# A GroupNorm streamed through one DMA queue: the pairs of stores and loads shifted by one tile

## The chip, the cores and the metric

The kernel runs on one core of a Trainium2 chip. The metric is the device time of one execution in microseconds (us); lower is better. The time before is the median of three runs.

## The reference

GroupNorm over `x` of shape (128, 1024, 32, 16) in bf16, with 32 groups of 32 channels:

```python
xr = x.reshape(B, G, C // G, H, W)          # 128, 32, 32, 32, 16
mu = xr.mean(axis=(2, 3, 4), keepdims=True)
var = ((xr - mu) ** 2).mean(axis=(2, 3, 4), keepdims=True)
xn = (xr - mu) / jnp.sqrt(var + 1e-5)
return xn.reshape(B, C, H, W) * g[None, :, None, None] + b[None, :, None, None]
```

Each of the 128 x 32 (sample, group) pairs has 32 x 512 = 16,384 values. The input is 134.2 MB and so is the output.

## The kernel before

**Tiles.** A tile holds 4 samples with all 32 groups: 128 partitions (one per sample and group) with 16,384 bf16 values each, 4.19 MB. There are 32 tiles (`NT`) and six buffers `xt0` to `xt5` (`NBUF`). Tile i uses buffer i mod 6. A tile is loaded into its buffer, scaled in place there, and stored from it.

**What is done with a tile.** The five engines each run a program of their own and meet through semaphores:

- TensorE (PE) adds the tile up: 32 matmuls with an identity matrix accumulate its 32 pieces of 512 columns in PSUM (line 148), after a wait for the load.
- VectorE (DVE) turns that into the negative mean (`mean`, line 165).
- ScalarE (ACT) computes the sum of squares in two activations over halves of the tile (line 278), then the standard deviation (lines 292 and 299).
- DVE makes the reciprocal, a scale and a bias for each channel (lines 179, 182, 189).
- DVE scales channels 0 to 13 in place and GpSimd (POOL) channels 14 to 31 (both line 218).

DVE's step for tile i begins with the mean of tile i + 1 and only then goes on to tile i:

```python
if i + 1 < NT:
    mean(i + 1, c + 3)
dve.reciprocal(out=col(rstd, i), in_=col(std, i))._wait_ge(...)
```

Engine instructions are issued in order, so the scaling of tile i also waits for the load of tile i + 1 and for its matmuls.

**What sets the order of the transfers.** All loads and stores of tiles are issued by SyncE (SP) on one queue, in the order of `sync_program`. SP issues them one after the other; where one has to wait, everything behind it in SP's program waits too. A store (line 123) waits until DVE and POOL have scaled the tile. A load (line 115) of tile n, from n = 6 on, waits until the store of tile n - 6 has landed, since it overwrites that buffer. The program first issues six loads, then goes through the stores in order; after each odd store (`RUN` is 2) it issues two loads.

Of the kernel before, what the change touches and what calls it, by code (L numbers as in the profile page):

```python
# [17 lines left out]
NBUF = 6  # L18
RUN = 2
# [5 lines left out]
def kernel(  # L25
# [15 lines left out]
    NT = B0 // NS  # L41
# [68 lines left out]
    def sync_program(sync):  # L110
        def load(i):
            j = i % NBUF
            if i >= NBUF:
                sync.wait_ge(st[j], 16 * (i // NBUF))
            sync.dma_start(out=xt[j][:], in_=x_v[i]).then_inc(ld[j], 16)

        for i in range(min(NBUF, NT)):
            load(i)
        for i in range(NT):
            j = i % NBUF  # L120
            sync.wait_ge(s_dve, i + 1)
            sync.wait_ge(s_pool, i + 1)
            sync.dma_start(out=o_v[i], in_=xt[j][:]).then_inc(st[j], 16)
            if i % RUN == RUN - 1:
                first = i + 1 + NBUF - RUN
                for n in range(first, min(first + RUN, NT)):
                    load(n)
        for j in range(NBUF):
            sync.wait_ge(st[j], 16 * len(range(j, NT, NBUF)))
# [179 lines left out]
    with tc.tile_critical():  # L309
        with nc.Block() as block:  # L310
            block.sync(sync_program)
            block.tensor(tensor_program)
            block.vector(vector_program)
            block.gpsimd(pool_program)
            block.scalar(scalar_program)
# [30 lines left out]
```

## Time and profile before

| | |
|---|---|
| median of 3 runs | 634.19 us (633.79 to 635.87) |
| the profiled execution | 634.93 us, its span 633.2 us |
| DMA queue of the tiles (q1) | 268.44 MB, 98.9% of the span |
| ACT busy | 476.5 us (75%) |
| POOL busy | 453.7 us (72%) |
| DVE busy | 348.3 us (55%) |
| PE busy | 259.3 us (41%) |
| a load, issue to landing | median 19.4 us (13.4 to 60.7) |
| a store, issue to landing | median 29.3 us (12.9 to 38.7) |

The span runs from the first to the last instruction in the profile; the device time holds 1.7 us more around it. Landing is when a transfer's completion reaches its semaphore. A transfer issued while others are queued waits for them, which is why most take two or three times as long to land as the queue needs for one. In a timeline of SP, a row gives the start of the first issue, the time to the end of the last issue of the row, and how many issues of one kind it merges.

### The profile page before, as it was taken

What the parts mean: (1) busy time and instruction counts of PE and PEld (TensorE: products, weight loads), DVE (VectorE), ACT (ScalarE), POOL (GpSimd) and SP (SyncE); (2) the same over time, 40 slices, a digit from 0 to 9 for tenths busy, and PEclk for the clock granted to TensorE, in tenths of its full rate; (3) what the DMA queues carried; (4) which work ended last, traced back from release to release, by engine and by line L of the source; (5) the groups of instructions that cost most, each with busy time, mean ns of one, the idle gap of its engine ahead of it and who ended that gap; (6) DMA issues with size and microseconds to landing.
All of it is one profiled execution on the core that took longest, in us unless ns stands there. A gap on an engine that the chain in (4) does not pass through costs nothing. (4 is left out here: it accounts for less than half of the span.)

```text
span 633.2 us, 3721 instructions
## 1 busy us (share of the span) xinstructions
PE 259.3 (41%) x1025; PEld 105.8 (17%) x1025; DVE 348.3 (55%) x610; ACT 476.5 (75%) x194; POOL 453.7 (72%) x583
## 2 busy tenths in 40 slices
PE   0977409054180632707327082360823608145000
PEld 0333103021030210302113031120301203012000
DVE  0057777767657175661757617476274762737660
ACT  0499999999959398693976939779397793967900
POOL 0049999999949398593986939769397693977990
PEclk9988858668595685957859577595765957659555
DMA  8999999999999999999999999999999999999986
GB/s 361 429 431 419 431 420 412 435 435 441 431 433 433 431 431 431 426 433 433 433 433 437 433 424 437 428 424 431 431 435 429 428 435 431 439 433 432 436 383 284
DMA packets 9324, 268.57 MB, mean 424 GB/s; under 512 B 1120, under 2 KB 1120, under 8 KB 1120
## 3 DMA queue, kind: packets, MB, share of 16 engines
q1 hardware_dynamic: 9216, 268.44, 98.9%
q8 instruction: 3, 0.05, 0.0%
q14 instruction: 9, 0.07, 0.0%
q10 hardware_dynamic: 96, 0.00, 0.0%
HBM read 134.22 MB, written 134.22 MB: 424 GB/s over the span
## 5 line engine op out<-in xcount | busy, mean ns | idle before, releaser
L218 POOL TENSOR_SCALAR xt<-xt,scl,bia 128x512 bf16<-128x512 bf16 x576 | 452.7, 801 | 163.6 <-DVE xt L218 163.6
L278 ACT ACTIVATE ja<-xt,negmean 128x8192 fp8e5<-128x8192 bf16 x64 | 455.5, 7118 | 123.4 <-DVE jd L165 121.9
L148 PE MATMUL pa<-xt,eye 128*128 128x512 bf16 x1024 | 259.1, 417 | 309.4 <-PEq L146 309.4
L218 DVE TENSOR_SCALAR xt<-xt,scl,bia 128x512 bf16<-128x512 bf16 x448 | 304.2, 753 | 1.2
L148 PEld LDWEIGHTS pa<-xt,eye 128*128 128x128 bf16 x1024 | 105.7, 105 | 462.4 <-issue 368.0
L165 DVE TENSOR_SCALAR_CACHE_REDUCE jd<-pa 128x512 bf16<-128x512 f32 x32 | 21.8, 681 | 165.3 <-PE pa L148 165.3
L179 DVE RECIPROCAL rstd<-std 128x1 f32<-128x1 f32 x32 | 5.2, 162 | 84.9 <-ACT std L299 84.9
L278 ACT ACTIVATION_READ_ACCUMULATOR ja<-xt,negmean 128x1 f32 x64 | 11.9, 186 | 0.0
L182 DVE TENSOR_SCALAR scl<-gb,rstd 128x32 f32<-128x32 f32 x32 | 10.2, 319 | 1.1
L299 ACT ACTIVATE std<-sq,half 128x1 f32<-128x1 f32 x32 | 9.4, 295 | 1.0
L189 DVE SCALAR_TENSOR_TENSOR bia<-scl,negmean,gb 128x32 f32<-128x32 f32 x32 | 8.5, 266 | 1.1
L292 ACT ACTIVATE half<-sq,eps_t 128x1 f32<-128x1 f32 x32 | 8.9, 278 | 0.0
L161 DVE COPY gb<-gb_p 128x64 f32<-128x64 f32 x1 | 0.2, 225 | 10.4 <-PE gb_p L134 10.4
L134 PE MATMUL gb_p<-gb_b,rep 32*128 32x64 bf16 x1 | 0.2, 231 | 11.4 <-DMA gb_b<-in_b_dram 11.4
L273 ACT ACT_TABLE_LOAD x1 | 1.3, 1283 | 1.9 <-issue 1.9
L165 DVE DVE_READ_ACCUMULATOR jd<-pa 128x1 f32 x32 | 2.5, 80 | 0.0
L134 PEld LDWEIGHTS gb_p<-gb_b,rep 32*128 32x128 bf16 x1 | 0.1, 100 | 11.4 <-DMA gb_b<-in_b_dram 11.4
L228 POOL TENSOR_SCALAR_AFFINE_SELECT eye<-ones_b 128x128 bf16<-128x128 bf16 x1 | 0.3, 295 | 0.9 <-DVE ones_b L160 0.9
L160 DVE MEMSET ones_b<- 128x128 bf16 x1 | 0.2, 165 | 1.1 <-SPq L309 1.1
L330 POOL MEMSET const-float32-0.0<- 128x1 f32 x1 | 0.1, 99 | 0.3 <-issue 0.3
L237 POOL TENSOR_SCALAR_AFFINE_SELECT rep<-ones_b 32x128 bf16<-32x128 bf16 x1 | 0.3, 305 | 0.0
L273 ACT ACTIVATE warm<-eps_t 128x1 f32<-128x1 f32 x1 | 0.2, 203 | 0.0
(4 smaller groups left out, 0.5 us busy)
## 6 DMA issues: line engine op xcount, KB each, us to landing
xt<-in_x_dram SPq DMA_DIRECT2D x32, 4096.0 KB, 19.4
out_dram<-xt SPq DMA_DIRECT2D x32, 4096.0 KB, 29.3
gb_b<-in_g_dram ACTq DMA_DIRECT2D x1, 2.0 KB, 6.5
gb_b<-in_b_dram ACTq DMA_DIRECT2D x1, 2.0 KB, 9.9
```

The source lines that it names most:

```text
L134: pe.matmul(out=gb_p[:].rearrange("p a k -> p (a k)"), lhsT=rep[:], rhs=gb_b[:].rearrange("q a k -> q (a k)"), start=True, stop=True,).the ...
L148: m = pe.matmul(out=pa[j][:], lhsT=eye[:], rhs=xt[j][:, k * MM_FREE : (k + 1) * MM_FREE], start=(k == 0), stop=(k == NMM - 1),)
L165: dve.tensor_scalar(out=jd[i % 2][:], in0=pa[i % NBUF][:], scalar1=-inv_n, scalar2=None, op0=ALU.mult, op1=ALU.add, accum_out=col(negmean, i),
L179: dve.reciprocal(out=col(rstd, i), in_=col(std, i))._wait_ge(s_std, c + 1).then_inc(s_dd, 1)
L182: dve.tensor_scalar(out=scl[j][:], in0=gam, scalar1=col(rstd, i), scalar2=None, op0=ALU.mult,)._wait_ge(s_dd, 3 * c + 2).then_inc(s_dd, 1)
L189: dve.scalar_tensor_tensor(out=bia[j][:], in0=scl[j][:], scalar=col(negmean, i), in1=bet, op0=ALU.mult, op1=ALU.add,)._wait_ge(s_dd, 3 * c ...
L218: return eng.tensor_scalar(out=span, in0=span, scalar1=scl[j][:, k : k + 1], scalar2=bia[j][:, k : k + 1], op0=ALU.mult, op1=ALU.add,)
L228: pool.affine_select(out=eye[:], in_=ones_b[:], pattern=[[-1, P]], compare_op=ALU.is_equal, fill=0.0, base=0, channel_multiplier=1,)._wait ...
L273: act.activation(out=warm[:], in_=eps_t[:], func=ACT.Sqrt)
L278: m = act.activation(out=ja[:], in_=xt[j][:, h * F // 2 : (h + 1) * F // 2], func=ACT.Square, bias=col(negmean, i), scale=1.0, accum_out=s ...
L292: act.activation(out=col(half, i), in_=sq[:, 2 * j : 2 * j + 1], func=ACT.Identity, bias=eps_t[:], scale=inv_n,)._wait_ge(s_sq, 3 * c + 1) ...
L299: act.activation(out=col(std, i), in_=sq[:, 2 * j + 1 : 2 * j + 2], func=ACT.Sqrt, bias=col(half, i), scale=inv_n,)._wait_ge(s_sq, 3 * c + ...
```

## The change

The runs of two stores and two loads begin one tile earlier: loads now follow the even stores instead of the odd ones. After store 0 comes one load (tile 6), after stores 1 and 2 come the loads of tiles 7 and 8, and so on; after stores 25 and 26 comes the last load, of tile 31. What a load and a store wait for is unchanged.

```diff
             sync.dma_start(out=o_v[i], in_=xt[j][:]).then_inc(st[j], 16)
-            if i % RUN == RUN - 1:
-                first = i + 1 + NBUF - RUN
-                for n in range(first, min(first + RUN, NT)):
+            if i % RUN == 0:
+                first = max(NBUF, i + 1 + NBUF - RUN)
+                for n in range(first, min(i + 1 + NBUF, NT)):
                     load(n)
```

The programs of the other four engines are the same in both kernels.

## The prediction

> **What bounds the kernel now.** I read the page's queue lines first, then the busy time of the engines, then SyncE's (SP's) timeline, and last the chain that ended last with a table of stretches.
>
> The queue lines say that one DMA queue carries all tiles and is full.
>
> ```profile
> DMA  8999999999999999999999999999999999999986
> GB/s 361 429 431 419 431 420 412 435 435 441 431 433 433 431 431 431 426 433 433 433 433 437 433 424 437 428 424 431 431 435 429 428 435 431 439 433 432 436 383 284
> q1 hardware_dynamic: 9216, 268.44, 98.9%
> ```
>
> All 64 transfers (32 loads, 32 stores, 4.19 MB each) go through q1, busy for 98.9% of the span; the busiest engine, ACT, has 75%. I write L for a load and S for a store, with the tile's number. The trace has the issue and the landing of each. L0 lands at 14.4 us and S31, the last, at 631.4. That is 63 intervals in 617.0 us, 9.79 on average; undisturbed neighbours are 9.67 apart (S0 at 74.0, S1 at 83.7). No interval exceeds 10.7. So the queue never runs dry from L0 to S31, and only its two ends, where the slices show 361, 383 and 284 GB/s, can hold anything else.
>
> A transfer can only be late if SP issues it late. This is SP at the start and at the end:
>
> ```profile
> 1.00 3.12 SPq L115 DMA_DIRECT2D xt<-in_x_dram  x6
> 54.39 15.35 SPq L123 DMA_DIRECT2D out_dram<-xt  x2
> 74.04 10.01 SPq L115 DMA_DIRECT2D xt<-in_x_dram  x2
> 84.41 15.36 SPq L123 DMA_DIRECT2D out_dram<-xt  x2
> ...
> 543.71 10.09 SPq L115 DMA_DIRECT2D xt<-in_x_dram  x2
> 553.90 64.97 SPq L123 DMA_DIRECT2D out_dram<-xt  x6
> ```
>
> S0 goes out at 54.4, S1 at 69.4. L6 needs the buffer that S0 reads; it goes out at 74.04, just as S0 lands, and L7 at 83.7, as S1 lands. While SP sits in a load's wait, the queue lives on what was issued before: at 74.0 that is S1 alone. This cover is what the change takes away at the start.
>
> The end is where compute shows. The chain that ended last begins at 563.2, as L30 lands:
>
> ```profile
> 563.28 8.98 PE pa L148 x32
> 572.26 0.02 issue
> 572.28 0.71 DVE jd L165 x2
> 573.00 0.02 issue
> 573.02 7.22 ACT ja L278 x2
> ```
>
> From there ACT takes 15 us for tile 30, 15 us more for tile 31, and POOL 14.15 us for tile 31 up to 618.5. S30 is issued at 603.5: **40.4 us from a tile's landing to its store's issue** (563.1 to 603.5). S31 is issued at 618.5 and lands 12.9 later. The stretches of the tail, whose columns after each engine's busy time are granted clock, DMA share and GB/s, show how close POOL and the queue finish:
>
> ```profile
> 560.00:605.00 45.00, 16.03 (x64) 6.60 (x64) 23.55 (x45) 34.22 (x16) 34.10 (x44) 0.69 1.01 435
> 605.00:615.00 10.00, 0.00 (x0) 0.00 (x0) 8.31 (x11) 0.00 (x0) 10.00 (x14) 0.50 0.95 410
> 615.00:620.00 5.00, 0.00 (x0) 0.00 (x0) 0.00 (x0) 0.00 (x0) 3.46 (x5) 0.50 0.56 242
> ```
>
> At 615 some DMA engines are through with S30 and idle at 242 GB/s in sum, while the slowest still works on it: S30 lands at 621.8, S31 at 631.4, a normal 9.6 apart. So the tail is just covered; the queue and the last tile's compute end together. Whatever comes later in either now adds to the time.
>
> **The change part by part.** No transfer is added or removed; PE, DVE, ACT and POOL keep their instructions. Only SP's order changes. Before, the order is L0 to L5, S0 S1 L6 L7, S2 S3 L8 L9, ..., S24 S25 L30 L31, S26 to S31. After, it is L0 to L5, S0 L6, S1 S2 L7 L8, ..., S23 S24 L29 L30, S25 S26 L31, S27 to S31.
>
> *Start.* L6 stands directly behind S0, so SP waits from 54.8 to 74.0 with S1 (ready at 69.4) queued behind that wait. When S0 lands the queue is empty. L6 goes out at 74.0 and must pay the whole latency of a lone transfer. Two rows price it: L0, issued into an empty queue, took 13.4 us to land; S31, issued with only a remnant ahead, took 12.9. So L6 lands at 86.9 to 87.4, where the stream before had its next landing at 83.7: a hole of 3.2 to 3.7 us. I take **3.5**, the middle, since L6 is a load like L0 but without the kernel's first instructions around it. A gain is excluded: an idle queue moves nothing, and the same 57 transfers follow. Nothing at all would be lost only if the slower DMA engines made up the hole; zero is the lower bound. S1 follows L6 at once, S2 (ready at 84.4) too.
>
> The Trainium skill has a rule for this price ("DMA: Bandwidth & Descriptors", Anatomy of one DMA): about 2.0 us fixed, plus the bytes at 436 GB/s, fitted on another issue path. By it a lone 4.19 MB transfer takes an estimated 11.6 us, the hole is 2.0 instead of 3.5, and the last store costs 1.3 less: 639.6 instead of 642.4. The rows are of this queue, so the sum stays with them.
>
> *Middle.* The pattern S S L L is the same, moved by one tile. When a load's wait ends, the other store of its pair is always in the queue, as before. Stores must be ready in time: in step i DVE takes the mean of tile i+1 before it scales tile i, so S(i) waits for L(i+1) too. Before, S25 was ready at 510.0 (its POOL work began at 495.84 and took 14.15) and was issued at 515.3, yet the queue ahead of it lasted to 543.7, when S24 landed. After, S26 stands to L27 exactly as S25 stood to L26. About 30 us of cover hide it; without them each pair would cost another 3.5. I cost it at nothing.
>
> *Tail.* Count landings. Before, L31 is number 58 and S26 number 59 (31 loads and 27 stores stand before S26's successor). After, S25 and S26 both stand ahead of L31, which becomes number 59 and lands where S26 did: 553.9 + 28.9 = 582.8, against 572.8. L30 lands one place earlier, which helps nobody: ACT has finished tile 30 before tile 31's mean exists. Tile 31 now takes the full path that tile 30 took, with PE idle for some 20 us before it as PE was before tile 30: 40.4 us. Its store goes out at 582.8 + 40.4 = 623.2, into a queue that is empty since S30 landed (621.8), and lands 12.9 later at 636.1: **4.7 later** than 631.4. If a lone transfer took only the 9.67 of a queued one this would be 1.4; with L0's 13.4 it is 5.2.
>
> S30 gets later too, since its scaling now waits for L31: L31's landing plus 25.3 (as S29 before: 563.1 to 588.4). Without the hole that is 608.1, and S29 lands at 612.1; S30 is queued in time, and S31 issues after it lands anyway.
>
> *Sum.* The hole moves every later landing, so both add: 582.8 + 3.5 + 40.4 + 12.9 = 639.6, less 631.4 is 8.2 us. The profiled execution took 634.93 (span 633.2), so 643.1; on the median of 634.19 it is **642.4**.
>
> **Rivals.**
> *The hole closes again.* When a few DMA engines lag (the 242 GB/s at 615 to 620 say that they do), a pause lets them start level, and the stream may win the 3.5 us back. Then the tail alone is left: 634.19 + 4.7 = 638.9. Against: a landing needs all 16 engines, and the slowest loses the hole like the rest.
>
> *Not slower: the stream has slack.* Intervals average 9.79 against the undisturbed 9.67. If the new order ran at 9.67 throughout, L31 would land at 14.4 + 58 x 9.67 + 3.5 = 578.8, S31 at 578.8 + 40.4 + 12.9 = 632.1: 634.9 in median, no change. It decides from a landing of L31 at 580.0 or earlier. Against: the two long stretches 90 to 330 and 330 to 560 us both ran at 431 GB/s, and the long intervals (10.0 to 10.7) are spread over the run, not bound to a place in the order that the change removes.
>
> *Each pair leaks.* If a store were not ready when SP reaches it and the queue ran out, each of the 12 groups would pay up to 3.5, 42 in all: 676; one or two of them 646 to 649. For: S25 had only 5 us between ready and issue. Against: the 30 us in the queue.
>
> **How the numbers follow.** The forecast has 0.68, the closing hole 0.15, the stream with slack 0.08 (0.05 no change, 0.03 faster), the leak 0.05, other slow causes 0.04. A difference under 0.3% (1.9 us) can't be told from none. Hence faster 0.03, same 0.05, slower 0.92. The range reaches down to 638.0, the rival at 638.9 less the 0.4 by which the lowest run lies under the median and some rounding, and up to 645.5: 642.4 with 3.7 for the hole, 13.4 for the last store, and the 1.7 by which the highest run lies over the median, plus 0.7 for a stream slower by 0.01 per interval.
>
> **What would show it.** Right: SP's timeline has S0 alone at 54.4, L6 at 74.0, then S1 and S2 behind it; L6 takes about 13 us to land; the first 5 us after 74 move far under 420 GB/s. The middle stays at 431. L31 is issued alone near 567, lands near 586, the chain that ended last begins there with 9 us of PE, has only one tile's ACT work, and POOL ends near 626.6; the slices of the last 15 us are emptier. Wrong: L6 landing under 10 us after S0, L31 landing before 580, stretches in the middle off 431 by more than 2%, or S31 landing less than 10 us after its issue.

## The result and the profile after

The changed kernel takes 643.35 us in median (642.58 to 644.23, four runs) against 634.32 (633.79 to 635.87, four runs): ratio 1.0137, 95% interval 1.0122 to 1.0152. It is slower, by 9.0 us in median; 642.4 was predicted. The profiled execution took 642.58, the lowest of the four, with a span of 640.7 against 633.2; what the trace explains is therefore 7.6 us of the 9.0; of the other executions (spans 641.0 to 642.4) there is no trace.

The queue lines of the changed kernel's page:

```profile
DMA  8999899999999999999999999999999999999976
GB/s 359 442 432 390 333 403 428 425 442 434 419 434 425 432 438 425 434 430 438 434 425 428 442 434 423 432 438 434 430 425 434 440 425 428 436 438 429 428 338 264
q1 hardware_dynamic: 9216, 268.44, 97.9%
```

Of before only the ends were below the rest. Now the fourth to sixth slices (48 to 96 us) are low too, 390, 333 and 403, and the last two are lower than they were. (The fourth ends before the change can act; in it load 5 landed 11.2 us after load 4 instead of 10.6.) Everything between is unchanged: the stretches 90 to 330 and 330 to 560 us ran at 431 and 432 GB/s, as before at 431 and 431.

SP's timeline of the changed kernel, start and end:

```profile
1.00 3.13 SPq L115 DMA_DIRECT2D xt<-in_x_dram  x6
54.31 0.35 SPq L123 DMA_DIRECT2D out_dram<-xt  x1
74.57 0.33 SPq L115 DMA_DIRECT2D xt<-in_x_dram  x1
75.00 9.54 SPq L123 DMA_DIRECT2D out_dram<-xt  x2
...
568.72 0.34 SPq L115 DMA_DIRECT2D xt<-in_x_dram  x1
569.15 59.14 SPq L123 DMA_DIRECT2D out_dram<-xt  x5
```

Store 0 goes out alone, load 6 follows only when store 0 has landed at 74.56, and store 1, ready at 69.2 (POOL has scaled it then), goes out behind it at 75.0. How that looks to the queue is seen in stretches of 3 us; first the kernel before, then the changed one (columns as before: busy time of the five rows, granted clock, DMA share, GB/s):

```profile
68.00:71.00 3.00, 3.00 (x16) 1.35 (x15) 2.29 (x7) 2.97 (x4) 2.13 (x3) 1.00 0.91 393
71.00:74.00 3.00, 0.55 (x3) 0.06 (x1) 3.00 (x5) 3.00 (x1) 3.00 (x5) 1.00 1.07 459
74.00:77.00 3.00, 0.00 (x0) 0.00 (x0) 3.00 (x5) 2.97 (x3) 3.00 (x5) 0.77 0.91 393
```

```profile
68.00:71.00 3.00, 3.00 (x13) 1.30 (x12) 2.31 (x7) 2.97 (x4) 2.13 (x3) 0.85 1.09 470
71.00:74.00 3.00, 2.78 (x13) 1.08 (x11) 3.00 (x5) 3.00 (x1) 3.00 (x5) 1.00 0.26 109
74.00:77.00 3.00, 0.00 (x0) 0.00 (x0) 3.00 (x5) 2.97 (x3) 3.00 (x5) 1.00 0.62 175
```

The hole begins soon after 71, not at 74.6: between 71 and 74 most of the 16 DMA engines run out of their share of store 0 and find nothing behind it (DMA share 0.26), while the slowest ones decide when it lands. Load 6 took 13.5 us to land.

At the end, the chain that ended last begins with load 31 instead of load 30 and holds one tile's ACT work instead of two:

```profile
588.29 6.72 PE pa L148 x24
...
595.07 1.69 PE pa L148 x7
...
596.78 0.71 DVE jd L165 x2
...
597.51 7.22 ACT ja L278 x2
604.74 0.02 issue
604.76 7.21 ACT ja L278 x2
...
620.27 7.62 POOL xt L218 x10
```

Load 31 lands at 588.2 and store 31 goes out at 628.0, 39.8 later. Store 30 has landed at 627.3 by then, and the queue is empty (columns as above):

```profile
615.00:620.00 5.00, 0.00 (x0) 0.00 (x0) 5.00 (x7) 0.00 (x0) 5.00 (x7) 0.50 1.00 433
620.00:625.00 5.00, 0.00 (x0) 0.00 (x0) 2.75 (x4) 0.00 (x0) 5.00 (x8) 0.50 0.58 249
625.00:630.00 5.00, 0.00 (x0) 0.00 (x0) 0.00 (x0) 0.00 (x0) 2.88 (x4) 0.50 0.26 111
```

From its issue store 31 took 12.9 us to land in the kernel before and takes 11.1 in the changed one (minimum, median and maximum are the same, since each row is of one transfer; the kernel before first):

```profile
DMA to landing us min/median/max: 12.9/12.9/12.9
DMA to landing us min/median/max: 11.1/11.1/11.1
```

Put side by side, the landings of both traces give the account (us; the positions are those of the 64 landings):

```
                                   before    after    later by
6 loads, store 0 (7th)              74.0      74.6     0.5   jitter of load 5, same order
8th: store 1 / load 6               83.7      88.1     3.8 more: 13.5 after store 0 instead of 9.7
59th: store 26 / load 31           582.8     588.2     1.0 more
63rd: store 30                     621.8     627.3     0.1 more
64th: store 31                     631.4     639.0     2.1 more: 11.8 after store 30 instead of 9.6
sum (of the unrounded steps)                           7.6
```

### The profile page after: what moved, and what is told of

Same layout as the page of the kernel before. It is cut to its first block, busy times and chain, and to the rows that moved or that the text cites. A ratio compares the mean times of both kernels' runs of the same rounds, so it can differ in the third digit from the quotient of the medians.

```text
span 640.7 us, 3704 instructions
## 1 busy us (share of the span) xinstructions
PE 257.6 (40%) x1008; PEld 106.1 (17%) x1025; DVE 345.6 (54%) x610; ACT 477.1 (74%) x194; POOL 451.7 (70%) x583
## 3 DMA queue, kind: packets, MB, share of 16 engines
q1 hardware_dynamic: 9216, 268.44, 97.9%
```

## The experiments

Five of them change the order of the transfers. These write the loop of SP with a list of the stores after which loads are issued, and only the list differs:

```diff
+        nxt = [NBUF]
         for i in range(NT):
...
-            if i % RUN == RUN - 1:
-                first = i + 1 + NBUF - RUN
-                for n in range(first, min(first + RUN, NT)):
-                    load(n)
+            if i in LOADS_AFTER:
+                while nxt[0] < min(i + 1 + NBUF, NT):
+                    load(nxt[0])
+                    nxt[0] += 1
```

The theory has two terms, a hole at the start and an uncovered last tile. Its rivals are that one of the two is the whole cost, or that the hole closes again on the way.

**The hole alone, first try.**

```diff
+LOADS_AFTER = [*range(0, 24, 2), 25]
```

> The changed kernel's start (load 6 directly behind store 0), but the end of the kernel before: one run of three stores 23 to 25 and three loads 29 to 31, so that load 31 has its old place, number 58 among the landings. Two-term theory: only the hole at 74 us is left, 3.8 us at load 6 plus 0.5 at store 0, about 638.3 in median, 1.005 to 1.008 of the kernel before. If the hole closes again on the way: 634.3, no change. If the hole is the whole cost: 643.3, as the changed kernel.

Measured: 643.89 against 634.41, ratio 1.0148 (1.0133 to 1.0162). My expectation was wrong, and at first sight the result speaks for the rival that the hole is everything. The trace says otherwise: the stream is as expected (store 30 lands at 626.6), but store 31 goes out only at 629.5. The chain that ended last shows why:

```profile
558.44 9.57 PE pa L149 x32
...
568.04 0.71 DVE jd L166 x2
...
568.77 7.22 ACT ja L279 x2
...
584.07 7.22 ACT ja L279 x2
...
591.32 7.21 ACT ja L279 x2
...
599.04 7.12 ACT ja L279 x2
...
606.18 7.21 ACT ja L279 x2
```

It begins with load 29, at 558.4. In the run of three, loads 29, 30 and 31 land 9.7 apart, and ACT needs 15 us for each tile. So ACT falls behind and finishes three tiles in a row: 558.3 + 40.4 + 2 x 15 = 628.7, against 629.5 measured. I had made a new, longer tail. The sum for the end needs this general form: for every k, store 31 goes out no earlier than about the landing of load k + 40.4 + 15 x (31 - k), which holds within a microsecond in these traces (39.8 instead of 40.4 in the changed kernel). The run of three belongs in the middle, and the test was made again (below).

**The tail alone.** Start as in the kernel before; a run of three in the middle brings the changed order in.

```diff
+LOADS_AFTER = [1, 3, *range(6, 27, 2)]
```

> The kernel before's start (stores 0 and 1 before load 6), one run of three (stores 4 to 6, loads 10 to 12) with which the order changes over to the changed kernel's, so that load 31 is number 59. Two-term theory: no hole, load 31 lands near 582.8, store 31 goes out near 622.6 to 623.2 and lands 11.1 to 12.9 later: 2.3 to 4.7 us over the kernel before, 636.6 to 639.0 in median. If the tail is covered and the hole is the whole cost: 634.3. If the tail is the whole cost: 643.3.

Measured: 637.43 against 634.41, ratio 1.0054 (1.0041 to 1.0067), 3.0 us. SP's timeline has the changed end:

```profile
562.71 0.34 SPq L115 DMA_DIRECT2D xt<-in_x_dram  x1
563.14 59.74 SPq L124 DMA_DIRECT2D out_dram<-xt  x5
```

Load 31 lands at 582.1, store 31 goes out at 622.55 (40.4 later) and lands 11.1 after that, at 633.6, where it landed at 631.4 before. Both rivals of a single cost fall here: the hole is not everything, and neither is the tail.

**The last tile split differently, in both kernels.** The edit is the same in each:

```diff
+LAST_SHARE = 18
...
-            for k in range(DVE_SHARE):
+            share = LAST_SHARE if i == NT - 1 else DVE_SHARE
+            for k in range(share):
                 m = scale_on(dve, j, k)
...
-            for k in range(DVE_SHARE, KC):
+            share = LAST_SHARE if i == NT - 1 else DVE_SHARE
+            for k in range(share, KC):
                 m = scale_on(pool, j, k)
-                if k == DVE_SHARE:
+                if k == share:
```

> The changed kernel, where in the last tile alone DVE scales 18 channels and POOL 14 (14 and 18 before). DVE then ends last: 18 x 0.68 = 12.2 us from a start 0.5 us ahead of POOL's, instead of POOL's 14.15, so store 31 goes out about 2.4 us earlier. Theory that the last tile's compute sets the end: 2.1 us less than the changed kernel (store 30's landing near 627.3 plus 9.7 stops the rest), about 641.2 in median. If the queue sets the end: 643.3, no gain.

> The kernel before with the same edit of the last tile. Theory that there the queue covers the last tile's compute (store 31 lands 9.6 us after store 30): no change, 634.3 in median, within 0.1%, although store 31 goes out some 2.4 us earlier. If the kernel before too was bound by its last tile: about 632.0.

Measured: the changed kernel falls to 640.37 (ratio to the kernel before 1.0092, 1.0079 to 1.0105), 3.0 under its 643.35; the kernel before stays at 634.88 against 634.41 (1.0009, 1.0001 to 1.0018). In the changed kernel store 31 goes out at 625.6, now ahead of store 30's landing at 626.4, and lands 10.2 after it. In the kernel before it goes out at 615.0 instead of 618.5 and lands 9.64 after store 30: it only waits longer in the queue. So the changed kernel ended with POOL's work on the last tile and the kernel before with the queue, which had covered it.

**The hole alone, again.**

```diff
+LOADS_AFTER = [0, 2, 4, *range(7, 26, 2)]
```

> The changed kernel's start again (load 6 directly behind store 0), with the change back to the order of the kernel before in the middle: one run of three stores 5 to 7 and three loads 11 to 13, and from there pairs that begin with even tiles, loads 30 and 31 being the last. Two-term theory: load 30 lands near 563.1 + 4.2 = 567.3, and two tiles of ACT work later store 31 goes out near 567.3 + 55.4 = 622.7, before store 30 has landed (near 626); the queue covers the tail, and the hole alone is left: 3.8 to 4.4 us, 638.2 to 638.8 in median. If the hole is the whole cost of the change: 643.3. If it closes on the way: 634.4.

Measured: 639.81 against 634.57, ratio 1.0087 (1.0074 to 1.0100), 5.2 us. SP's timeline of this kernel has the old end:

```profile
548.68 10.15 SPq L115 DMA_DIRECT2D xt<-in_x_dram  x2
558.92 64.60 SPq L124 DMA_DIRECT2D out_dram<-xt  x6
```

Store 31 goes out at 623.2, before store 30 lands at 626.8, and lands 9.7 after it. So the tail is covered again and the start alone costs 5.2, about a microsecond more than expected. In the trace, load 6 lands 13.2 after store 0 (3.6 over 9.67), and from there to store 30 the same 55 intervals take 539.1 us instead of 538.1. The changed kernel has the same surplus (539.2). The four traces with a hole at the start (the changed kernel, its 18-to-14 form and both tries of the hole alone) lie between 538.9 and 539.3, the four without a hole (the kernel before, its 18-to-14 form and the two kernels of the tail alone) between 537.1 and 538.1. So the hole does not close, and the stream behind it is 1 to 2 us slower. Why, no run shows. In this kernel the two stores of a pair mostly land about 9.93 and 9.76 after what precedes them, where it is mostly near 9.67 in the kernel before; but the kernel before has the wider spacing too, from store 22 on, and so the hole is not its only cause.

The records of single packets in the traces bear on the rival of the closing hole. A transfer has 144 packets (9216 for the 64 transfers): 128 of 32 KB, which run 16 at a time in eight rounds, and one of 4 bytes at the end on each of the 16 DMA engines. In the kernel before, these last 16 packets start within 2.4 us of each other at store 0 and within 6.8 us at store 30: the engines drift apart. With the hole this spread falls from 2.8 us at store 0 to 0.6 at load 6, so the engines do start level after the pause, as the rival said. But they drift apart again, to 6.8 us at store 30, and no time is won.

The tail's 3.0 and the start's 5.2 add to 8.2, within the interval of the whole (7.7 to 9.6 us, from 1.0122 to 1.0152); by the ratios, 0.54% and 0.87% add to 1.41%, and the whole is 1.37%.

**Eight holes.**

```diff
+LOADS_AFTER = [*range(1, 26, 2), 8, 12, 16, 20]
```

> The kernel before, with four of its pairs in the middle (stores 8 and 9, 12 and 13, 16 and 17, 20 and 21) taken apart into store, load, store, load: at each of these eight loads SP waits for a store with nothing queued behind it. If every hole costs what a lone load does (13.4 to 13.5 us to landing against 9.67): 8 x 3.8 = 30 us, 664.5 in median. If the stream wins holes back: under 645. By a fixed cost of 2.0 us a hole: 650.5.

Measured: 663.46 against 634.57, ratio 1.0463 (1.0448 to 1.0478): 28.9 us, 3.6 a hole. SP's timeline shows two of them; each load goes out as the store ahead of it lands:

```profile
230.51 0.33 SPq L115 DMA_DIRECT2D xt<-in_x_dram  x1
230.94 0.38 SPq L124 DMA_DIRECT2D out_dram<-xt  x1
253.60 0.33 SPq L115 DMA_DIRECT2D xt<-in_x_dram  x1
```

All eight loads land 13.2 to 13.4 us after the store ahead of them. That is 29.0 us over eight usual intervals, and the medians differ by as much, so the holes stay. (The profiled execution, the lowest of the four, ends 27.4 us later than that of the kernel before.) The first hole found the engines 3.0 us apart and the second 0.6, and the two loads landed 13.4 us after their stores alike. The surplus that followed the hole at the start is not seen here: the other 32 intervals from store 8 to store 30 average 9.76 us, against 9.79 for that stretch in the kernel before. So it is no fixed part of a hole's price.

The Trainium skill's fixed cost ("DMA: Bandwidth & Descriptors", Anatomy of one DMA), about 2.0 us on top of the bytes, is fitted on another issue path. It is too small for a load that enters this empty queue, which showed 3.5 to 3.8 us over the usual 9.67.

**The tail alone, and the last tile split 18 to 14.** The kernel of the tail alone with the edit of the last tile.

> The kernel with the changed tail but no hole, and in it the last tile scaled 18 channels on DVE and 14 on POOL. Theory that the tail's cost is nothing but the time by which the last tile's compute outlasts store 30: store 31 goes out near 620, before store 30 lands (621.2), the queue covers it, and the whole cost is gone: 634.4 to 634.9 in median. If a load's later place costs by itself: 637.4, as without the edit.

Measured: 634.96 against 634.57, ratio 1.0016 (1.0004 to 1.0027). Store 31 goes out at 620.6, before store 30 lands at 621.7. The tail's cost of 3.0 is down to 0.4 in median (0.3 to 1.7 by the interval): a later place of load 31 costs little or nothing by itself as long as the queue has store 30 to move.

**A store into the empty queue.** What stayed open was why the last store took 11.1 us to land alone, but a load 13.2 to 13.5.

```diff
             sync.wait_ge(s_pool, i + 1)
+            if i in EMPTY_BEFORE:
+                sync.wait_ge(st[(i - 1) % NBUF], 16 * ((i - 1) // NBUF + 1))
             sync.dma_start(out=o_v[i], in_=xt[j][:]).then_inc(st[j], 16)
```

> The kernel before, where stores 9, 13, 17 and 21 also wait until the store ahead of them (8, 12, 16, 20) has landed: four times a store, not a load, enters an empty queue, and a load (whose own wait is then over) is issued right behind it. This separates two readings of why a load into the empty queue took 13.2 to 13.5 us and the last store 11.1. If stores are quicker to start than loads: 11.1 us to landing, 4 x 1.4 = 6 us in all, 640 in median. If a transfer with another issued behind it takes longer than one alone: 13.4 us, 4 x 3.7 = 15 us, 649.

Measured: 649.49 against 634.94, ratio 1.0232 (1.0215 to 1.0249), 14.6 us in all, near the number of the second reading. But neither reading holds alone: the four stores land 12.1 us after their issue, between both. The four holes themselves hold 4 x (12.16 - 9.68) = 9.9 us; the rest of the 14.2 between the two profiled executions' landings of store 31 (645.6 against 631.4) is spread over later intervals.

Where in a transfer the difference sits can be read from its packets. The last store of the kernel, alone in the queue (three traces), has eight rounds of 1.22 to 1.25 us in the mean. The four stores with a load behind them have the same in seven rounds, and 1.9 us in the eighth. A load that enters the empty queue with a store behind it (load 6 in four traces and the eight loads of the eight holes) takes 1.8 to 2.0 us for the first round and 2.1 to 2.2 for the eighth. So such a load is slow to begin, and both are slow to end when a transfer of the other kind stands behind them. Load 0, which has a load behind it, begins slowly too (1.9) but ends at 1.21; that the kind of the follower matters rests on this one transfer. What in the chip slows these rounds is not shown.

None of these kernels beats the one before. The kernel of the tail alone comes back to it (634.96) when the last tile is covered again.

## Why the prediction was right

The time, its sign and both mechanisms came as forecast. By its steps:

- **The start**: SP's order, the lone store 0 and the hole are there, in the rows named. Sized 3.5, it measured 3.8 at load 6. A further 1.1 us in the stream behind it, which the sum did not have, has no cause that the runs show. The lower bound of zero, and with it the rival of the closing hole, fell with the start alone at 5.2 and eight holes at 3.6 each.
- **The middle**, costed at nothing: no store was late, and the bytes per second of the two long stretches are the same. The rival of leaking pairs did not occur.
- **The tail**: load 31 as the 59th landing, and 40.4 us from there to the last store (39.8; 40.4 with the tail alone), hold. The mis-sized term is the last store's landing. I took 12.9 from store 31 of before as the price of a lone transfer, but that store was issued 3.3 us before store 30 had landed, so part of the 12.9 was waiting. Alone it takes 11.1. The tail was therefore 2.2 in the trace with the tail alone (3.0 in median) instead of 4.7.
- **The sum** of 8.2 is near the 9.0 because the two errors have opposite signs: by the medians of the two parts, a start too cheap by 1.7 (5.2 instead of 3.5) and a tail too dear by 1.7 (3.0 instead of 4.7). That they cancel is luck, and the total alone would not have shown either.
- **The stream with slack** was the rival that ended in no change. It needed load 31 by 580.0; it landed at 588.2, and the stream after the hole ran slower rather than at its 9.67.
- **Two slips** in the working change nothing in the forecast. The count of 31 loads and 27 stores is what stands ahead of load 31 after the change; ahead of store 26 before stand 32 loads and 26 stores. And 12 leaking groups would add their 42 us to the 642.4, not to the time before: 684, not 676.

The Trainium skill's figure would have given an estimated 639.6. Its fixed 2.0 us lies between what this queue showed for a lone store (11.1 to landing, 1.4 over the usual 9.67) and for a load (3.5 to 3.8 over).

## What to carry to other kernels

Where one queue carries both directions and a load waits for a store to land, something else must stand in the queue behind that store; count, for every such wait in the issue order, what is queued at that moment. At the end, compare for each of the last loads its landing plus the compute behind it with the queue's own end: the order is free as long as the queue ends later. To price an exposed transfer, take a row of the same kind of transfer whose queue was really empty when it was issued.

## What the runs showed of the hardware

A queue runs dry in part before its last transfer has landed: when store 0 stood alone, the 16 DMA engines finished it up to 2.7 us apart, and they moved 109 GB/s between 71 and 74 us, just ahead of its landing at 74.6, against 459 in the same stretch with store 1 behind it. In a full queue the engines drift apart (last packets within 1.3 us of each other at load 0 and 6.8 at store 30 of the kernel before). A drained queue sets them level again (0.6 to 0.7 us at load 6), and that won no time. From issue to landing with an empty queue, a store took 11.1 us with nothing behind it and 12.1 with a load behind it; a load with a store behind it took 13.2 to 13.5. The surplus sits in single rounds of packets: the first of a load, the last where a transfer of the other kind stands behind.
